# Rounding the first weight blocks by integer steps on three engines, with two split copies and a split sketch product, in a polysketch-attention and ELU kernel

## The chip, the cores and the metric

The kernel runs on one core of one Trainium2 chip. The metric is device time in microseconds, the median of several runs. The engines go by the names of the profile: PE (TensorE, with PEld for its weight loads), DVE (VectorE), ACT (ScalarE), POOL (GpSimd) and SP (SyncE, which issues most DMAs). Each takes its instructions in the order in which the program gives them.

## What is computed

```python
def phi(x):                                  # for q and k
    a = np.einsum('rd,bhsd->bhsr', S1, x)    # r = 8 sketch rows
    b = np.einsum('rd,bhsd->bhsr', S2, x)
    return outer(a, b)                       # 64 features per token
kv, z = phi(k)^T v, sum over s of phi(k)
attn = (phi(q) kv) / (phi(q) z + 1e-6)       # B = 4, H = 4, S = 1088, D = 32
x = attn as (4352, 128)                      # tokens x (heads * D)
h = x @ w_in                                 # 128 -> 2048
out = where(h > 0, h, exp(min(h, 0)) - 1) @ w_out
```

S1, S2, w_in and w_out come to the chip as 64-bit floats, two 32-bit words per value. The kernel makes 32-bit floats of them on the chip: this is the rounding that the change is about.

## The kernel before

The tokens are worked in groups of 512 (`g`), and w_in and w_out in eight blocks of 256 features (`cp`). For each pair the step is: h = x by w_in (`mm1`, 16 instructions into two PSUM tiles), e = exp on ACT (`elu_a`), gg = the ELU on DVE (`elu_d`), then gg by w_out (`mm2` and other forms of it for later groups). Groups 0 and 1 run interleaved while later inputs are still on their way; in `steps` the order is (0,0), (0,1), (1,0), (1,1), and so on. The schedule is manual: the program's order of calls is each engine's order of instructions, and the stretch that matters here, up to the first steps, is written out call by call at the end of the function.

The queries take this way to x, for groups 0 and 1:

- Sketch product: the transposed queries `qT` (a DVE transpose, L280) by the sketch matrix. Group 0 has `q1_first` (tile abqp, L505) and `q1z_first` (zqp, L517, the part for the denominators). Group 1 has `q1_second` (abwp, L526): eight products of 96 columns, on PE as sixteen instructions, and one ACT copy to the tile abw (L530). Both group-1 halves need the second DVE transpose of qT (128x576).
- `q2` = `q2_den` (pw, the sum and reciprocal den, an; L586 to L596) and `q2_out` (qp, in two halves, L609), all on DVE. `q2_den` takes a function `between` that is called after pw, and `q2_out` one between its halves; these slots hold the first step of a rounding (`RA`).
- `q4_early`: eight PE transposes of qp into two PSUM tiles qtp (L621), each copied by ACT to qpT (L622, 512 columns).
- `q5_early`: qpT by kvS, sixteen PE instructions into two PSUM tiles xps (L628), each copied by ACT to its half of the columns of xg (L634, 256 columns).

kvS, the attention state of batch 0, comes from `KA(0)` (kv, L435) and `KS_first` (an ACT copy kd, L481, a PE transpose, L482, an ACT copy kvS, L483). `keep_warm` issues PE products of constants into a tile that nobody reads.

Rounding of a block, in order: `RA` (DVE, L102: sign and mantissa masked away from the upper word, into W), `RB` (ACT, L107: the exponent rebased), `RS`, `RM`, `RD`, `RE` (all DVE, L117, L121, L129, L137: sign put in, mantissa of the upper word as a number, the lower word added to it, and the product of mantissa and exponent). `order` numbers the blocks: block 0 is w_in of cp 0, block 1 w_in of cp 1, block 2 w_out of cp 0. For blocks 0 and 1 the middle steps run once over both (`RC_2`). h of (0, 0) needs block 0, h of (0, 1) block 1, and the first product into the output tile o (`mm2(0, 0)`, L256) block 2, whose rounding `RA(2)`, `RB(2)`, `RC(2)` is written among the first steps.

The order around the change, after it `mm1_first` (h of group 0, block 0, in two halves of the columns w, as the halves of xg arrive):

```python
q2(1, 2, lambda: RA(2))
RB(2)
elu_a(0, 0, 0)
elu_a(0, 0, 1, (0,))
mm1(0, 1, (0,))
q4_early(1)
elu_d(0, 0, 0)
mm1(0, 1, (1,))
elu_a(0, 0, 1, (1,))
RC(2)
...
q5_early(1)
elu_d(0, 0, 1)
mm2(0, 0, True, False)
```

SP issues the loads in the order S1, k, q, v, w_in block 0, the rest of q, block 1, the two first w_out blocks, and the others. The functions that the diff touches, with the line numbers of the profile:

Of the kernel before, what the change touches and what calls it, by code (L numbers as in the profile page):

```python
# [12 lines left out]
F32 = mybir.dt.float32  # L13
ALU = mybir.AluOpType
U32 = mybir.dt.uint32
MUL, ADD, SUB, MAX = ALU.mult, ALU.add, ALU.subtract, ALU.max
AND, OR, SHL = ALU.bitwise_and, ALU.bitwise_or, ALU.logical_shift_left
EXP = mybir.ActivationFunctionType.Exp
RELU = mybir.ActivationFunctionType.Relu
AX = mybir.AxisListType.X  # L20


def _ap(ap: bass.AP, free):
    return dataclasses.replace(ap, ap=[list(ap.ap[0])] + [list(x) for x in free])
# [3 lines left out]
def kernel(  # L28
# [21 lines left out]
    nc = tc.nc  # L50
    B, H, S, D = q.shape
    R = S1.shape[0]
    P = 128
# [10 lines left out]
    const = ctx.enter_context(tc.tile_pool(name="const", bufs=1))  # L64
    work = ctx.enter_context(tc.tile_pool(name="wk", bufs=2))
    psum = ctx.enter_context(tc.tile_pool(name="psum", bufs=2, space=bass.MemoryType.PSUM))
# [27 lines left out]
    nc.vector.memset(ebias[:], -float(896 << 23))  # L94
    tiny = const.tile([P, 1], F32, name="tiny")
    nc.gpsimd.memset(tiny[:], 2.0 ** -20)

# [4 lines left out]
    def round_b(raw, dst, eng=nc.scalar):  # L104
        d = dst.bitcast(U32)
        if eng is nc.scalar:
            nc.scalar.activation(d, d, RELU, scale=8.0, bias=ebias[:dst.shape[0]])  # L107
        else:
# [3 lines left out]
    def words(raw):  # L112
        return (raw[:, :, 0], raw[:, :, 1]) if len(raw.shape) == 3 else (raw[:, :, :, 0], raw[:, :, :, 1])
# [5 lines left out]
    def round_m(raw, dst):  # L119
        hi = words(raw)[1]  # L120
        nc.vector.tensor_scalar(hi, hi, 0x000FFFFF, 0x00100000, op0=AND, op1=OR)  # L121

    def round_c(raw, dst):
        round_s(raw, dst)
        round_m(raw, dst)
# [15 lines left out]
    wide = S1.dtype != F32  # L141
# [12 lines left out]
    nc.vector.memset(warm[:], 0.0)  # L154
    nc.scalar.activation(warm[:], warm[:], EXP)

    W = const.tile([P, NP, 4 * P], F32, name="W")
    raw_w = {}
    if wide:
        raw_2 = const.tile([P, 2, 4 * P, 2], U32, name="raw")  # L160
# [18 lines left out]
    def round_w(f, i, *a):  # L179
        if wide:  # L180
            cp, w_in, w_out = order[i]
            c = slice(0 if w_in else 2 * P, 4 * P if w_out else 2 * P)
            f(raw_w[cp][:, c], W[:, cp, c], *a)

    def RA(i):
        round_w(round_a, i)

    def RB(i):
        round_w(round_b, i)


    def RC_2():
        if wide:
            for f in (round_s, round_m, round_d):
                f(raw_2[:, :, :2 * P], W[:, :2, :2 * P])

    def RS(i):
        round_w(round_s, i)
# [7 lines left out]
    def RE(i):  # L206
        round_w(round_e, i)
# [43 lines left out]
    width = [32]  # L251
# [8 lines left out]
    def keep_warm(n, cols=256, tile=P):  # L260
        ones = nc.const_aps.tensor(1.0, [P, 256], F32)
        for i in range(n):
            for c in range(0, P, tile):
                nc.tensor.matmul(idle[c:c + tile, :cols], ones[:, :tile], ones[:, :cols], skip_group_check=True,  # L264
                                 tile_position=(0, c))
# [222 lines left out]
    abw, ans, qp, qpT, xg, xps = {}, {}, {}, {}, {}, {}  # L488
# [7 lines left out]
    def half_tile(g, k):  # L496
        return (g // 2, 8 * (g % 2) + k) if g < NQ - 1 else (k, NT - 1)
# [20 lines left out]
                                 qT[b][:, t, :], SW[:, :, 2, :], skip_group_check=True, tile_position=(0, 64 * u))  # L518
        return p[:, :128].rearrange("p (t h r) -> p h t r", t=4, h=H)

    def q1_second():
        p = psum.tile([P, 512], F32, name="abwp", tag="h", bufs=4)
        for i in range(4):
            for u in range(2):
                b, t = half_tile(1, 2 * i + u)
                nc.tensor.matmul(p[64 * u:64 * u + 64, i * 96:i * 96 + 96], qT[b][:, t, :],  # L526
                                 SW[:].rearrange("p h x r -> p (h x r)"), skip_group_check=True,
                                 tile_position=(0, 64 * u))
        abw[1] = work.tile([P, H * 4, 3 * R], F32, name="abw1", tag="abq1", bufs=1)
        nc.scalar.copy(abw[1][:].rearrange("p (h t) y -> p h t y", h=H),  # L530
                       p[:, :384].rearrange("p (t h y) -> p h t y", t=4, h=H))


    units = {g: ([g, g + 1] if 4 <= g < NQ - 1 else [g]) for g in [2, 3] + list(range(4, NQ, 2))}
    un = {g: sum(qn[x] for x in gr) for g, gr in units.items()}
# [41 lines left out]
    def q2(g, parts=1, between=None):  # L577
        q2_den(g, None, between)
        q2_out(g, parts)

    def q2_den(g, zq=None, between=None):
        m = H * (un[g] if g > 1 else qn[g])
        x = abw[g][:, :m, :]
        pw = pws[g % 2]
        if zq is None:
            nc.vector.tensor_mul(pw[:, :m, :R], x[:, :, R:2 * R], x[:, :, 2 * R:3 * R])  # L586
        else:
            nc.vector.tensor_mul(pw[:, :m, :R].rearrange("p (h t) r -> p h t r", h=H),
                                 x[:, :, R:2 * R].rearrange("p (h t) r -> p h t r", h=H), zq)
        if between:  # L590
            between()
        den = work.tile([P, 8 * H], F32, name="den", tag="den")
        nc.vector.tensor_reduce(den[:, :m], pw[:, :m], axis=AX, op=ADD)
        nc.vector.reciprocal(den[:, :m], den[:, :m])
        an = work.tile([P, 8 * H, R], F32, name="an", tag="an")
        nc.vector.tensor_mul(an[:, :m], x[:, :, R:2 * R], _ap(den[:, :m], [[1, m], [0, R]]))  # L596
        ans[g] = an

    def q2_out(g, parts=1, between=None):
        m = H * qn[g]  # L600
        x, an = abw.pop(g), ans.pop(g)
        qp[g] = work.tile([P, 4 * H, R, R], F32, name="qp", tag="qp", bufs=2)
        for i in range(parts):
            if i and between:
                between()
            h = slice(i * m // parts, (i + 1) * m // parts)
            a_ = an[:, h]
            b_ = x[:, h, :R]
            nc.vector.tensor_mul(qp[g][:, h], _ap(a_, list(a_.ap[1:]) + [[0, R]]),  # L609
                                 _ap(b_, [b_.ap[1], [0, R], b_.ap[2]]))  # L610

    def q4_early(g):

        qpT[g] = work.tile([P, H, 2, P], F32, name="qpT", tag="qpT", bufs=2)
        for hh in range(2):
            p = psum.tile([P, 512], F32, name="qtp", tag="aux")
            for h2 in range(2):
                for m in range(2):
                    o = (h2 * 2 + m) * P
                    r = (2 * hh + h2) * 4 + 2 * m  # L620
                    nc.tensor.transpose(p[:, o:o + P], qp[g][:, r:r + 2].rearrange("p t i j -> p (t i j)"), ident[:])  # L621
            nc.scalar.copy(qpT[g][:, 2 * hh:2 * hh + 2], p[:].rearrange("p (h m s) -> p h m s", h=2, m=2))  # L622

    def q5_early(g):
        xp = [psum.tile([P, 512], F32, name="xps", tag="aux") for _ in range(2)]
        for h in range(H):
            for w in range(2):
                nc.tensor.matmul(xp[w][D * h:D * h + D, :256], kvS[64 * w:64 * w + 64, h, :],  # L628
                                 qpT[g][64 * w:64 * w + 64, h].rearrange("p m s -> p (m s)"),
                                 skip_group_check=True, tile_position=(64 * w, D * h))  # L630
        xg[g] = work.tile([P, 512], F32, name="xg", tag="xg", bufs=3)
        to = xg[g][:].rearrange("p (m w s) -> p w m s", w=2, s=P)
        for w in range(2):
            nc.scalar.copy(to[:, w], xp[w][:, :256].rearrange("p (m s) -> p m s", s=P))  # L634


    exch = [raw_2[:, c].bitcast(F32).rearrange("p (e m a) w -> p e m (a w)", e=2, a=16) if wide else
# [206 lines left out]
        for c in cs:  # L844
            quarters(hs[g, cp][c][:, :n], W[:, cp, c * P:c * P + P], xg[g][:, :n])

    def mm1_first():
        hs[0, 0] = [psum.tile([P, 512], F32, name="h", tag="h", bufs=4) for c in range(2)]
        for w in range(2):
            for c in range(2):  # L850
                cols = [x[:].rearrange("p (m w s) -> p w m s", w=2, s=P)[:, w] for x in (hs[0, 0][c], xg[0])]
                quarters(cols[0], W[:, 0, c * P:c * P + P], cols[1])

    def elu_a(g, cp, c, parts=(0, 1)):
# [5 lines left out]
        if 0 in parts:  # L860
            nc.scalar.activation(e, hs[g, cp][c][:, :n], RELU, scale=-1.0)  # L861
        if 1 in parts:
            nc.scalar.activation(e, e, EXP, scale=-1.0)  # L863

# [44 lines left out]
    def elu_last_a(k, parts=(0, 1)):  # L909
# [3 lines left out]
        if 0 in parts:  # L913
            nc.scalar.activation(e, hs["last", k][:, :2 * P], RELU, scale=-1.0)
        if 1 in parts:
            nc.scalar.activation(e, e, EXP, scale=-1.0)

# [39 lines left out]
    KO_first(7, KT)  # L957
    keep_warm(1, 96, 64)
    zq = q1z_first()
    q2_den(0, zq, lambda: RA(0))  # L960
    q2_out(0, 2, lambda: RA(1))
    KA(0)
    KS_first()
    keep_warm(1)
    RB(0)
    RB(1)
    q4_early(0)
    transp(qT, "q", 0, 8, NT)
    RC_2()
    RE(0)  # L970
    RE(1)
    q1_second()
    q5_early(0)
    keep_warm(1, 192, width[0])
    mm1_first()
    q2(1, 2, lambda: RA(2))
    RB(2)
    elu_a(0, 0, 0)
# [129 lines left out]
    for n in range(2, N):  # L1108
        g, cp = steps[n]
# [29 lines left out]
        g, cp = before  # L1139
# [10 lines left out]
    g = NQ - 2  # L1150
# [53 lines left out]
```

## Time and profile before

| what | us |
|---|---|
| median of 3 runs (lowest to highest) | 262.14 (261.85 to 262.18) |
| span of the profiled execution, first to last instruction | 260.57 |
| median less that span: what lies around it | 1.57 |
| PE, DVE, ACT, POOL busy in the span | 254.8, 186.9, 183.4, 159.0 |
| first h (`mm1_first`) on PE | 16.25 |
| group 1's pw on DVE | 16.35 |
| first product into o on PE | 21.58 |

The profile shows one execution. A timeline row gives the start, the time that the row takes, the engine, the line, the operation, the tiles written and read, the shape, and how many instructions are merged in it; in brackets stands the idle time of the engine ahead of the row and what ended it. [...]

### The profile page before, as it was taken

The page shows a single profiled execution, that of the slowest core. Times are in us where ns is not written, and L with a number is a line of the kernel's source. Part 1 is how long each engine was busy: PE and PEld are TensorE (multiplying, and loading weights), DVE is VectorE, ACT ScalarE, POOL GpSimd, SP SyncE. Part 2 cuts the span into 40 slices and gives each one's busy share as a digit, 9 for nine tenths or more (in the row PEclk, how much of TensorE's full clock was granted, in tenths as well). Part 3 has the DMA queues.
Part 4 walks back from the last instruction along what each step waited for, and adds up shares of the span by engine and source line. Part 5 has one row for each costly group of instructions (what it writes and reads, how often), then busy time and mean ns, then how long its engine had stood idle before and what let it go on. Part 6 is the DMA issues. An engine that isn't in the chain of part 4 may idle for free.

```text
span 260.6 us, 9756 instructions
## 1 busy us (share of the span) xinstructions
PE 254.8 (98%) x4123; PEld 158.4 (61%) x4123; DVE 186.9 (72%) x352; ACT 183.4 (70%) x358; POOL 159.0 (61%) x202
## 2 busy tenths in 40 slices
PE   8899999999999999999999999999999999999994
PEld 6753333453346667666666666665666666668993
DVE  6799999999988967997477675744466746544651
ACT  2379968766667577776687777775877777777792
POOL 3520007002179996788678798888688888887310
PEclk9999999999999999999999999999999999999999
DMA  5998079012112210002100204220001110110021
GB/s 173 330 358 222 3 223 268 24 21 85 28 18 28 31 34 18 3 15 34 20 0 4 33 10 104 60 30 13 3 3 27 34 26 3 25 19 3 3 30 33
DMA packets 30379, 15.61 MB, mean 60 GB/s; under 512 B 22496, under 2 KB 28000, under 8 KB 30336
## 3 DMA queue, kind: packets, MB, share of 16 engines
q1 hardware_dynamic: 29904, 14.63, 23.0%
q8 instruction: 32, 0.52, 0.9%
q10 hardware_dynamic: 368, 0.30, 0.3%
q0 software_dynamic: 64, 0.07, 0.1%
q14 instruction: 11, 0.09, 0.1%
HBM read 11.31 MB, written 2.36 MB: 52 GB/s over the span
## 4 chain that ended last, share of the span: by engine, by line
PE 97%; DVE 1%; ACT 0%; issue 0%; DVEq 0%
PE h L256 45%; PE pb L790 17%; PE pa L790 13%; PE o L256 5%; PE pb L766 4%; PE ol L256 3%; PE idle L264 1%; PE kv L435 1%; PE abp L343 1%; PE h L681 1%; PE h L551 1%; PE qtp L621 1%; DVE qp L609 1%; PE h L693 1%; PE xps L628 0%; PE kfps L365 0%
## 5 line engine op out<-in xcount | busy, mean ns | idle before, releaser
L256 PE MATMUL h<-xg,W 128*32 128x512 f32 (+3 forms) x904 | 130.8, 539 | 0.4 <-ACT xg L634 0.4
L869 DVE SCALAR_TENSOR_TENSOR gg<-e,h 128x512 f32<-128x512 f32 x128 | 85.9, 681 | 52.6 <-ACT e L863 47.8
L861 ACT ACTIVATE e<-h 128x512 f32<-128x512 f32 x128 | 75.5, 590 | 46.2 <-PE h L256 46.0
L863 ACT ACTIVATE e<-e 128x512 f32<-128x512 f32 x128 | 80.9, 632 | 3.8
L751 POOL TENSOR_TENSOR tt<-gg 128x512 f32<-128x512 f32 x50 | 64.3, 1286 | 28.9 <-DVE gg L869 25.2
L256 PEld LDWEIGHTS h<-xg,W 128*32 128x32 f32 (+1 forms) x904 | 43.0, 122 | 43.0 <-issue 34.4
L754 POOL TENSOR_TENSOR tt<-gg,tt 128x256 f32<-128x256 f32 x50 | 36.9, 739 | 3.9
L753 POOL TENSOR_TENSOR tt<-tt,gg 128x256 f32<-128x256 f32 x50 | 36.7, 734 | 3.9
L790 PEld LDWEIGHTS pa<-gg,W 128*64 128x64 f32 (+1 forms) x496 | 23.7, 126 | 22.4 <-issue 22.2
L790 PE MATMUL pa<-gg,W 128*64 128x128 f32 (+1 forms) x496 | 30.6, 274 | 0.0
L790 PE MATMUL pb<-tt,SS 128*64 128x128 f32 (+1 forms) x480 | 29.6, 273 | 0.0
L790 PEld LDWEIGHTS pb<-tt,SS 128*64 128x64 f32 (+1 forms) x480 | 22.8, 126 | 0.0
L790 PE MATMUL pa<-tt,SS 128*32 128x128 f32 (+1 forms) x288 | 21.2, 273 | 0.0
L790 PE MATMUL pb<-gg,SS 128*64 128x128 f32 (+1 forms) x256 | 19.9, 273 | 0.0
L790 PE MATMUL pb<-tt,W 128*64 128x128 f32 (+1 forms) x256 | 19.9, 273 | 0.0
L134 POOL TENSOR_TENSOR raw<-raw,tiny 128x512 f32<-128x512 f32 x1 | 1.0, 1041 | 24.7 <-DVE raw L129 24.7
L256 PE MATMUL o<-gg,W 128*32 128x512 f32 x128 | 15.3, 595 | 0.0
L790 PEld LDWEIGHTS pa<-tt,SS 128*32 128x32 f32 (+1 forms) x288 | 13.7, 124 | 0.0
L790 PEld LDWEIGHTS pb<-gg,SS 128*64 128x64 f32 (+1 forms) x256 | 12.8, 125 | 0.0
L790 PEld LDWEIGHTS pb<-tt,W 128*64 128x64 f32 (+1 forms) x256 | 12.8, 125 | 0.0
L766 PE MATMUL pb<-gg,W 128*32 128x256 f32 x192 | 11.5, 380 | 0.0
L921 DVE SCALAR_TENSOR_TENSOR gg<-e,h 128x256 f32<-128x256 f32 x16 | 6.6, 418 | 6.4 <-PE h L256 3.2
(163 smaller groups left out, 269.3 us busy)
## 6 DMA issues: line engine op xcount, KB each, us to landing
raw<-in_moe_w_in_dram SPq DMA_DIRECT2D x8, 256.0 KB, 6.3
raw<-in_moe_w_out_dram SPq DMA_DIRECT2D x8, 256.0 KB, 6.5
out_dram<-ob SPq DMA_DIRECT2D x112, 16.0 KB, 1.5
hd_k<-in_k_dram SPq DMA_DIRECT2D x3, 544.0 KB, 7.5
hd_q<-in_q_dram SPq DMA_DIRECT2D x3, 544.0 KB, 8.5
v<-in_v_dram SPq DMA_DIRECT2D x4, 288.0 KB, 7.1
v<-in_v_dram SPq DMA_DIRECT2D x4, 256.0 KB, 8.4
raw<-qpF SPq DMA_DIRECT2D x16, 64.0 KB, 2.0
```

What stands on the lines that cost most here:

```text
L256: nc.tensor.matmul(dst[c:c + tile], lhs[:, c:c + tile], rhs, skip_group_check=True, tile_position=(0, c), **kw)
L264: nc.tensor.matmul(idle[c:c + tile, :cols], ones[:, :tile], ones[:, :cols], skip_group_check=True, tile_position=(0, c))
L343: nc.tensor.matmul(ps[i // 5][64 * u:64 * u + 64, 64 * (i % 5):64 * (i % 5) + 64], kT[b][:, u * KT + i, :], Sab[:].rearrange("p h y -> p ( ...
L751: nc.gpsimd.tensor_tensor(_ap(t[:, 0], [[4 * P, 2], [P, 2], [1, P]]), _ap(gs[g, cp][:, 0, P:], [[4 * P, 2]] + us), _ap(gs[g, cp][:, 0], [[ ...
L753: nc.gpsimd.tensor_tensor(t[:, 1], t[:, 2], b11, op=ADD)
L754: nc.gpsimd.tensor_tensor(t[:, 3], b21, t[:, 1], op=SUB)
L766: nc.tensor.matmul(acc[1][0][r:r + width[0], 256 * hi:256 * hi + 256], lhs[:, w:w + width[0]], gg[:, c, 256 * u:256 * u + 256], start=(cp ...
L790: nc.tensor.matmul(bank[r:r + width[0], P * col:P * col + P], lhs[:, w:w + width[0]], rhs[:, u], start=(first and i in ((0,) if g == 1 els ...
L861: nc.scalar.activation(e, hs[g, cp][c][:, :n], RELU, scale=-1.0)
L863: nc.scalar.activation(e, e, EXP, scale=-1.0)
L869: nc.vector.scalar_tensor_tensor(gs[g, cp][:, c, :n], es[g, cp][:, c, :n], -1.0, hs[g, cp][c][:, :n], op0=ADD, op1=MAX)
L921: nc.vector.scalar_tensor_tensor(gs["last", k // 2][:, k % 2, :2 * P], es["last", k // 2][:, k % 2, :2 * P], -1.0, hs["last", k][:, :2 * P ...
```

## The change

For blocks 0 and 1 the rounding is replaced. With hi and lo the two words of a value, it is now: `strip`, hi without its sign into W (DVE for block 0, ACT's Abs for block 1); `floor`, the maximum of that and a small constant (POOL); `shift`, three bits to the left (DVE); `low`, lo scaled by 2^-51 plus 2.0, whose bits are the exponent's offset and the rounded low mantissa bits (ACT); `whole`, the integer sum of the two (POOL); and `round_s`, the sign (DVE, as before). `RA`, `RB`, `RC_2` and `RE` of these two blocks go.

The second copy of `q4_early(0)` is made by ACT and DVE, 256 columns each, and the second of the two copies of `q5_early(0)` by DVE. `q1_second` is cut in two: its first half stands after `q5_early(0)`, its second half and the one copy to abw stand inside `mm1_first`, between its two halves. The last `keep_warm` ahead of `mm1_first` has 64 columns instead of 192.

```diff
+    two = const.tile([P, 1], F32, name="two")
+    nc.gpsimd.memset(two[:], 2.0)
...
+    def strip(raw, dst, eng=nc.vector):
+        if eng is nc.vector:
+            nc.vector.tensor_scalar(dst.bitcast(U32), words(raw)[1], 0x7FFFFFFF, None, op0=AND)
+        else:
+            nc.scalar.activation(dst, words(raw)[1].bitcast(F32), ABS)
+
+    def floor(raw, dst):
+        nc.gpsimd.tensor_scalar_max(dst, dst, 2.0 ** -15)
+
+    def shift(raw, dst):
+        nc.vector.tensor_scalar(dst.bitcast(U32), dst.bitcast(U32), 3, None, op0=SHL)
+
+    def low(raw, dst):
+        lo = words(raw)[0]
+        nc.scalar.activation(lo.bitcast(F32), lo, IDENTITY, scale=2.0 ** -51, bias=two[:dst.shape[0]])
+
+    def whole(raw, dst):
+        nc.gpsimd.tensor_tensor(dst.bitcast(U32), dst.bitcast(U32), words(raw)[0], op=ADD)
...
-    def RC_2():
-        if wide:
-            for f in (round_s, round_m, round_d):
-                f(raw_2[:, :, :2 * P], W[:, :2, :2 * P])
+    R1 = round_w
...
-    def q1_second():
-        p = psum.tile([P, 512], F32, name="abwp", tag="h", bufs=4)
-        for i in range(4):
+    def q1_second(tiles):
+        if 1 not in abw:
+            abw[1, 0] = psum.tile([P, 512], F32, name="abwp", tag="h", bufs=4)
+            abw[1] = work.tile([P, H * 4, 3 * R], F32, name="abw1", tag="abq1", bufs=1)
+        p = abw[1, 0]
+        for i in tiles:
...
+        if 3 in tiles:
+            nc.scalar.copy(abw[1][:].rearrange("p (h t) y -> p h t y", h=H),
+                           p[:, :384].rearrange("p (t h y) -> p h t y", t=4, h=H))
...
-    def q4_early(g):
+    def q4_early(g, split=False):
...
+            if split and hh:
+                nc.scalar.copy(qpT[g][:, 2], p[:, :2 * P].rearrange("p (m s) -> p m s", m=2))
+                nc.vector.tensor_copy(qpT[g][:, 3], p[:, 2 * P:].rearrange("p (m s) -> p m s", m=2))
...
-            nc.scalar.copy(to[:, w], xp[w][:, :256].rearrange("p (m s) -> p m s", s=P))
+            (nc.vector.tensor_copy if split and w else nc.scalar.copy)(
+                to[:, w], xp[w][:, :256].rearrange("p (m s) -> p m s", s=P))
...
-    def mm1_first():
+    def mm1_first(between):
         hs[0, 0] = [psum.tile([P, 512], F32, name="h", tag="h", bufs=4) for c in range(2)]
         for w in range(2):
+            if w:
+                between()
...
     zq = q1z_first()
-    q2_den(0, zq, lambda: RA(0))
-    q2_out(0, 2, lambda: RA(1))
+    R1(strip, 0)
+    R1(floor, 0)
+    R1(low, 0)
+    q2_den(0, zq)
+    R1(strip, 1, nc.scalar)
+    R1(floor, 1)
+    R1(low, 1)
+    q2_out(0, 2)
+    for i in range(2):
+        R1(shift, i)
+        R1(whole, i)
     KA(0)
     KS_first()
     keep_warm(1)
-    RB(0)
-    RB(1)
-    q4_early(0)
+    q4_early(0, True)
     transp(qT, "q", 0, 8, NT)
-    RC_2()
-    RE(0)
-    RE(1)
-    q1_second()
-    q5_early(0)
-    keep_warm(1, 192, width[0])
-    mm1_first()
+    R1(round_s, 0)
+    q5_early(0, True)
+    R1(round_s, 1)
+    q1_second((0, 1))
+    keep_warm(1, 64, width[0])
+    mm1_first(lambda: q1_second((2, 3)))
     q2(1, 2, lambda: RA(2))
```

More of the change, by code (lines that the diff above doesn't have):

```diff
@@ L18 @@
 EXP = mybir.ActivationFunctionType.Exp
+IDENTITY = mybir.ActivationFunctionType.Identity
+ABS = mybir.ActivationFunctionType.Abs
 RELU = mybir.ActivationFunctionType.Relu
@@ L528, in q1_second @@
                                  tile_position=(0, 64 * u))
-        abw[1] = work.tile([P, H * 4, 3 * R], F32, name="abw1", tag="abq1", bufs=1)
-        nc.scalar.copy(abw[1][:].rearrange("p (h t) y -> p h t y", h=H),
-                       p[:, :384].rearrange("p (t h y) -> p h t y", t=4, h=H))
+        if 3 in tiles:
+            nc.scalar.copy(abw[1][:].rearrange("p (h t) y -> p h t y", h=H),
+                           p[:, :384].rearrange("p (t h y) -> p h t y", t=4, h=H))
     units = {g: ([g, g + 1] if 4 <= g < NQ - 1 else [g]) for g in [2, 3] + list(range(4, NQ, 2))}
@@ L621, in q4_early, with q5_early @@
                     nc.tensor.transpose(p[:, o:o + P], qp[g][:, r:r + 2].rearrange("p t i j -> p (t i j)"), ident[:])
-            nc.scalar.copy(qpT[g][:, 2 * hh:2 * hh + 2], p[:].rearrange("p (h m s) -> p h m s", h=2, m=2))
-    def q5_early(g):
+            if split and hh:
+                nc.scalar.copy(qpT[g][:, 2], p[:, :2 * P].rearrange("p (m s) -> p m s", m=2))
+                nc.vector.tensor_copy(qpT[g][:, 3], p[:, 2 * P:].rearrange("p (m s) -> p m s", m=2))
+            else:
+                nc.scalar.copy(qpT[g][:, 2 * hh:2 * hh + 2], p[:].rearrange("p (h m s) -> p h m s", h=2, m=2))
+    def q5_early(g, split=False):
         xp = [psum.tile([P, 512], F32, name="xps", tag="aux") for _ in range(2)]
```

## The prediction

> **What bounds the kernel now.** I read the page's parts 1 and 2 first. TensorE (PE) is busy for 98% of the span, and the granted clock has full height in every slice.
>
> ```profile
> span 260.6 us, 9756 instructions
> ...
> PE 254.8 (98%) x4123; PEld 158.4 (61%) x4123; DVE 186.9 (72%) x352; ACT 183.4 (70%) x358; POOL 159.0 (61%) x202
> ```
>
> So a change helps only if it takes idle time or work away from PE, and it hurts wherever it makes PE wait. The change lies between 9 and 18 us, so next I read the PE timeline there, then that of VectorE (DVE), in which the small share 72% hides a stretch that is full.
>
> ```profile
> 13.34 0.63 PE L621 MATMUL qtp<-ident,qp 128*128 128x128 f32 x4 [0.24 <-DVE qp L609]
> 13.93 0.88 PE L526 MATMUL abwp<-SW,qT 128*64 128x96 f32 x16
> 14.74 0.66 PE L628 MATMUL xps<-qpT,kvS 64*32 64x256 f32 x16
> 15.34 0.53 PE L264 MATMUL idle<-const-float32-1.0 128*32 128x192 f32 x8
> 16.25 2.79 PE L256 MATMUL h<-xg,W 128*32 128x256 f32 x40 [0.38 <-ACT xg L634]
> 18.97 1.09 PE L621 MATMUL qtp<-ident,qp 128*128 128x128 f32 x8
> 19.99 1.06 PE L256 MATMUL h<-xg,W 128*32 128x512 f32 x8
> 20.99 0.66 PE L628 MATMUL xps<-qpT,kvS 64*32 64x256 f32 x16
> 21.58 1.92 PE L256 MATMUL o<-gg,W 128*32 128x512 f32 x16
> ```
>
> Up to 16.25 PE follows a chain (qp, transposes, x, h). From 16.25 on no row has idle time before it: PE is the bound to the end.
>
> ```profile
> 12.50 0.69 DVE L609 TENSOR_TENSOR qp<-an,abq 128x512 f32<-128x512 f32 x1
> ...
> 15.68 0.76 DVE L137 SCALAR_TENSOR_TENSOR W<-raw,W 128x256 f32<-128x256 f32 x2
> 16.35 0.29 DVE L586 TENSOR_TENSOR pw<-abw 128x128 f32<-128x128 f32 x1
> ...
> 17.70 1.29 DVE L609 TENSOR_TENSOR qp<-an,abw 128x512 f32<-128x512 f32 x2
> ...
> 20.97 0.43 DVE L137 SCALAR_TENSOR_TENSOR W<-raw,W 128x256 f32<-128x256 f32 x1
> ```
>
> DVE is as full as PE: it is busy without a gap from 10.34 to 28.9. Its pw of group 1 (L586) starts when the rounding ends (16.44, less the usual overlap of 0.09), not when its input comes, which was there at 15.34 (ACT's copy L530, 14.86 + 0.48). The last view is the list of waits between 8 and 24 us, and its decisive line is a small one:
>
> ```profile
> PEld o L256 <- DVE W L137: 0.4, 1, 0.4
> ```
>
> The first product into o (21.58) needs the w_out block whose rounding ends on DVE at 20.97 + 0.43 = 21.40. Its weight load waited for that, while PE was still in xps. **PE and DVE meet here without slack**: what makes DVE late between 16.35 and 21.40 arrives on PE nearly undiminished.
>
> **The change, part by part.** Times are of the profiled execution: span 260.57, where the runs have 262.14 in the median. The 1.57 between lies around the span, and I carry it along.
>
> *qp of group 0.* RA(0) and RA(1) leave DVE. The reduction L593 began at 10.75 and could begin at 10.63 + 0.03: −0.09. The second L609 began at 12.50 instead of 12.30: −0.20. strip(0) (0.29, the row of L102 with the same form; block 0 has landed by 9.43) lies in the 0.23 in which L588 waited for PE, plus one overlap: 0. So qp ends at 12.90 instead of 13.19.
>
> *ACT's new work.* low(0), strip(1), low(1) stand ahead of the copy kd (L481), which ran at 11.43 after 1.90 us idle. Block 1 lands at 10.94 by my count: the queue reuses eight landing marks in turn, and its issue at 10.96 is the eighth after block 1's (5.23). Abs isn't in the trace; it lies between a 256-column copy (L634: two in 0.65, so 0.28 from start to start) and L107 (two in 0.91, so 0.40). I take the copy, since neither has a bias tile. low has L107's form: 0.51. strip(1) runs from 10.97, low(1) 11.25 to 11.76, kd from 11.70: +0.27 (with the other end +0.39, with a later landing more). The idle time doesn't cover this, because it was idle time before a landing. kd leads to PE's transpose, kvS and then, in PE's order, the qtp transposes: the first four move from 12.44 to 12.71, the second four, one every 0.109, follow at 13.20 and end at 13.80, instead of 13.96. Of the 0.29 won on DVE 0.16 is left.
>
> *The split copies.* The second qpT copy took ACT 0.59; two halves take 0.37 there and 0.28 to 0.42 on DVE (L938, 128 columns from PSUM; L921, 256 columns: I take 0.42, the same width). ACT ends the first copy at 14.0 and its half at 14.28, DVE its own at 14.25, instead of 14.59: −0.31. xps follows 0.16 behind: 14.44 to 15.11. The first xg half is copied from 15.20 to 15.57, and the second no longer stands between it and h: that and the above give h at 15.67 instead of 16.25, **−0.58**. DVE runs the q transpose to 15.0, round_s(0) to 15.3 and its xg half to 15.7, which h's second part needs at 16.9. The dropped keep-warm columns lie in PE's waiting time: 0.
>
> *Rounding.* RC_2 and two RE (0.65 + 0.43 + 0.69 + 0.76) leave DVE; two shifts (0.17 at L110's 16x32 to 0.29; I take 0.29) and two round_s (0.42, L117 at this width) come. On GpSimd (POOL) floor lies between 0.23 (L304, 64 columns) and 0.74 (L753, two inputs); from L304 to the 0.29 of 128 columns (masks) it grows by 0.06 per 64: I take 0.41. whole lies between 0.66 (half of L135, which also reads every other word) and 1.31; I take 0.74: whole(0) ends near 13.9, whole(1) near 14.7. W isn't late until whole(0) ends after 15.15, so both ends cost nothing. Sxp, SWs, qE and zh now stand behind these four on POOL and end near 17; the first to need any is kfps at 37.4. No DMA moves.
>
> *The sketch product of group 1 (q1_second).* Before, it ran at 13.93, under the wait for qpT. Now its first half follows the q transpose at 15.0, its second half stands behind h's first part (0.86), and the one copy to SBUF waits for both. So: h 15.67, + 0.86 = 16.53, + 0.55 for eight of the sixteen (0.30 of starts + 0.25) = 17.08, + 0.03 and the copy 0.48 = 17.59, + 0.03: pw at 17.62 instead of 16.35, **+1.27**. This is the wait that the change adds. Behind pw on DVE stand, in order, RA(2), den, an, both qp, elu_d and the whole rounding of block 2; RB(2) on ACT and all after it follow RA(2). DVE, eased by some 0.7 us, idles from about 16.1 to 17.6.
>
> *On PE.* h and the eight other products keep it busy to 18.6. The qtp of group 1 needs the first qp, 18.40 + 1.27 = 19.67, so PE idles 1.1 us. h resumes at 20.93 (+0.94). The product into o needs block 2, 21.40 + 1.27 = 22.67, 0.18 more as before: 22.85, **+1.27**. ACT, gapless from 18.4 to 32.3, has the same delay. Nothing later gives it back, as PE has no idle row there. With some hundredths absorbed I take +1.25: span 261.8, time 262.14 + 1.25 = **263.4**. The ends (kd 0.12 later or 0.1 earlier; pw reached 0.3 sooner or later) give 263.0 to 263.9 for this case.
>
> **A rule against the row.** L117 with 512 columns took 1.72 at 44.26, 0.67 elsewhere:
>
> ```profile
> 44.26 1.72 DVE L117 SCALAR_TENSOR_TENSOR W<-raw,W 128x512 uint32<-128x512 uint32 x1
> ```
>
> ```profile
> 42.81 2.62 POOL L322 TENSOR_TENSOR kp<-abk 128x1280 f32<-128x1280 f32 x1
> ```
>
> It ended 0.55 after POOL's long instruction (45.43), so it seems to have stood still until then. The Trainium skill, "SBUF — State Buffer", section "Who interferes with whom", says as much: a DVE instruction with two SBUF inputs and a GpSimd instruction that reads SBUF exclude each other, and the second waits for all of the first. That speaks against floor(1), as the next rival shows.
>
> **Rivals.** (1) *POOL gets in first.* floor(1) is ready at about 11.35 while an runs (11.29 to 11.58), and both qp have two SBUF inputs. If POOL starts between an and qp, qp waits up to 0.41: qp ends at 13.31, the second qtp start at 13.45 instead of 13.20: +0.25, time 263.65. For it: the row above. Against: DVE queues its next instruction 0.03 behind the last. (2) *The late product is hidden: faster.* Then only h's −0.58 is left: 261.6. This decides at one point: ACT's abw copy would have to end by 15.8, and it stands behind h's first part. For it: DVE has less to do. Against: the rows give 17.6. (3) *No change*: pw is reached some 0.9 sooner than I reckon, and what DVE loses is caught up: about 262.2. (4) *An operation is dear.* A POOL integer add above 1.9 us pushes h, 3 us each giving about +1.1 more: 264.5. Or Abs or Identity makes ACT reload its table: the trace has one load, 1.28 us at 2.06, and Copy, Relu and Exp need no second. Two loads (there and back), one ahead of low(0), mostly hidden by the wait for the landing, one ahead of the exponential, give about +1.3 more: 264.7. The Trainium skill, "ScalarE: Activation LUTs", section "Table sets", counts both functions among those that every set holds, which would leave no load.
>
> **How the numbers follow.** Forecast 0.60, (1) 0.19, (4) 0.06: all slower. (3) 0.08; (2) 0.07. 0.2% is 0.52 us, about what a measurement here tells from nothing. Faster 0.07, same 0.08, slower 0.85. The range goes from 262.5 to 264.2: it holds the forecast, (1) and the upper part of (3), and leaves out (2), (4) and the rest of (3), under 2 in 10.
>
> **What would show it.** The first h near 15.7 (range 15.4 to 16.0); before the pw of group 1 an idle DVE of about 1.5 us, ended by ACT's abw copy; a PE gap near 1.1 us before the second qtp, released by qp; the first product into o near 22.85, and the same PE rows behind it. kd near 11.7 shows the landing; an L609 longer than 0.7 shows rival (1). The prediction is wrong if pw starts before 17.0, or if o starts at 21.6 although pw is late.

## The result, and the profile after

| | before | after |
|---|---|---|
| median of 5 runs (lowest to highest), us | 261.85 (261.73 to 262.18) | 263.58 (263.49 to 264.27) |
| ratio, 95% interval | | 1.0067 (1.0055 to 1.0080) |
| span of the profiled execution | 260.57 | 261.85 |

The change makes the kernel slower by 0.7%, 1.73 us between the medians. The first view is the PE timeline of the changed kernel over the stretch that was shown of before (lines moved down by 20 to 26: L276 is h and o, L549 abwp, L643 qtp, L654 xps).

```profile
12.41 1.03 PE L643 MATMUL qtp<-ident,qp 128*128 128x128 f32 x8
13.68 1.40 PE L654 MATMUL xps<-qpT,kvS 64*32 64x256 f32 x16 [0.24 <-ACT qpT L648]
15.10 0.55 PE L549 MATMUL abwp<-SW,qT 128*64 128x96 f32 x8
15.58 0.32 PE L284 MATMUL idle<-const-float32-1.0 128*32 128x64 f32 x8
15.72 1.05 PE L276 MATMUL h<-xg,W 128*32 128x256 f32 x16
16.70 0.55 PE L549 MATMUL abwp<-SW,qT 128*64 128x96 f32 x8
17.18 1.93 PE L276 MATMUL h<-xg,W 128*32 128x256 f32 x24
20.00 1.23 PE L643 MATMUL qtp<-ident,qp 128*128 128x128 f32 x8 [0.89 <-DVE qp L631]
21.16 1.07 PE L276 MATMUL h<-xg,W 128*32 128x512 f32 x8
22.16 0.66 PE L654 MATMUL xps<-qpT,kvS 64*32 64x256 f32 x16
22.75 1.92 PE L276 MATMUL o<-gg,W 128*32 128x512 f32 x16
```

h starts 0.53 sooner than before (15.72 instead of 16.25), and yet o starts 1.17 later (22.75 instead of 21.58). The 0.53 is not the change's. This execution was ahead by 0.59 already at zqp, a product that the change doesn't touch (before, then after):

```profile
9.57 0.66 PE L517 MATMUL zqp<-SW,qT 128*64 128x32 f32 x16 [0.17 <-DVE SW L465]
8.98 0.66 PE L537 MATMUL zqp<-SW,qT 128*64 128x32 f32 x16 [0.17 <-DVE SW L485]
```

Counted from zqp, h takes 6.74 instead of 6.68, and o 13.77 instead of 12.01. That is 1.76 more, about the 1.73 between the medians. Between h and o stands what the kernel before did not have: PE idles 0.89 ahead of the second qtp, until DVE has qp of group 1. The DVE timeline shows why qp is late:

```profile
13.94 0.42 DVE L646 COPY qpT<-qtp 128x256 f32<-128x256 f32 x1 [0.94 <-ACT qpT L645]
...
15.61 0.47 DVE L121 SCALAR_TENSOR_TENSOR W<-raw,W 128x256 uint32<-128x256 uint32 x1
17.81 0.29 DVE L608 TENSOR_TENSOR pw<-abw 128x128 f32<-128x128 f32 x1 [1.73 <-ACT abw L553]
...
22.26 0.42 DVE L160 SCALAR_TENSOR_TENSOR W<-raw,W 128x256 f32<-128x256 f32 x1
```

pw of group 1 waits 1.73 us for ACT's copy of the sketch product; before, it waited for nothing. It starts 1.46 later, qp of group 1 follows it, and the second qtp starts at 20.00 instead of 18.97. From there to o the PE timeline has no idle time: the h behind that qtp starts 1.17 later (21.16 instead of 19.99), and o has the same 1.17.

The rounding of block 2 (L160) ends at 22.68 instead of 21.40, 0.07 ahead of o (0.18 before). In the list of waits the weight load of o still has the row it had before:

```profile
PEld o L276 <- DVE W L160: 0.4, 1, 0.4
```

This row doesn't show that block 2 held o. It is the same 0.4 in e3 and e8 below, where pw came sooner than before, and in every kernel here o starts 0.59 to 0.60 behind the xps just ahead of it.

From the start of o to the end there are 239.11 us after and 238.99 before. All of the loss lies ahead of o, in the first 23 us.

### The profile page after: what moved, and what is told of

It reads as the page before. It is cut to its first block, busy times and chain, and to the rows that moved or that the text cites. A ratio compares the mean times of both kernels' runs of the same rounds, so it can differ in the third digit from the quotient of the medians.

```text
span 261.9 us, 9762 instructions
## 1 busy us (share of the span) xinstructions
PE 254.7 (97%) x4123; PEld 157.9 (60%) x4123; DVE 186.4 (71%) x352; ACT 183.4 (70%) x358; POOL 162.1 (62%) x207
## 4 chain that ended last, share of the span: by engine, by line
PE 92%; DMA 2%; SPq 2%; ACT 1%; DVE 1%; issue 0%
PE h L276 44%; PE pb L817 17%; PE pa L817 13%; PE o L276 5%; PE pb L793 4%; PE ol L276 3%; DMA raw<-in_moe_w_in_dram 2%; PE kv L455 1%; PE h L708 1%; SPq L81 1%; PE h L573 1%; PE qtp L643 1%; PE h L720 0%; PE kfps L385 0%; PE xps L654 0%; SPq L89 0%
## 5 line engine op out<-in xcount | busy, mean ns | idle before, releaser
L276 PE MATMUL h<-xg,W 128*32 128x512 f32 (+3 forms) x904 | 131.0, 539 | 0.0
L276 PEld LDWEIGHTS h<-xg,W 128*32 128x32 f32 (+1 forms) x904 | 42.8, 122 | 42.3 <-issue 34.6
L276 PE MATMUL o<-gg,W 128*32 128x512 f32 x128 | 15.4, 595 | 0.0
```

Of the source, the lines that this page charges most:

```text
L276: nc.tensor.matmul(dst[c:c + tile], lhs[:, c:c + tile], rhs, skip_group_check=True, tile_position=(0, c), **kw)
```

## The experiments

Theory: the late sketch product of group 1 makes the loss, through pw on DVE. Rivals: the new rounding makes it (A), or the split copies are what matters (B). Each kernel was timed beside the kernel before, whose median in these comparisons was 261.85 to 261.93. Executions don't all start alike (the last section), so times inside the profile are also read from zqp, a product ahead of all that the kernels differ in, and from kd, ACT's copy at the head of the chain to x. "o to end" is nearly the same in all of them. "zqp to o", less the 12.01 of before, gives what the medians give within 0.13, but for e7, whose profiled execution was the slowest of its five runs.

| kernel | zqp | kd | first h | pw | first o | zqp to o | o to end | median | ratio to before (95%) |
| --- | --- | --- | --- | --- | --- | --- | --- | --- | --- |
| before | 9.57 | 11.43 | 16.25 | 16.35 | 21.58 | 12.01 | 238.99 | 261.85 | |
| changed | 8.98 | 11.51 | 15.72 | 17.81 | 22.75 | 13.77 | 239.11 | 263.58 | 1.0067 (1.0055 to 1.0080) |
| e1 | 8.87 | 11.42 | 15.96 | 16.45 | 21.39 | 12.52 | 239.08 | 262.35 | 1.0025 (1.0011 to 1.0039) |
| e2 | 9.10 | 10.97 | 15.79 | 17.90 | 22.84 | 13.74 | 239.10 | 263.71 | 1.0066 (1.0054 to 1.0078) |
| e3 | 8.95 | 11.41 | 15.70 | 15.15 | 21.03 | 12.08 | 238.97 | 261.90 | 1.0004 (0.9993 to 1.0014) |
| e4 | 9.68 | 12.50 | 16.37 | 18.45 | 23.39 | 13.71 | 239.08 | 263.56 | 1.0059 (1.0046 to 1.0072) |
| e5 | 9.35 | 11.22 | 15.70 | 15.15 | 21.14 | 11.79 | 239.09 | 261.68 | 0.9992 (0.9983 to 1.0001) |
| e6 | 8.89 | 11.48 | 17.07 | 17.02 | 22.40 | 13.51 | 239.02 | 263.28 | 1.0056 (1.0044 to 1.0069) |
| e7 | 8.89 | 11.93 | 17.14 | 17.10 | 22.48 | 13.59 | 239.01 | 262.94 | 1.0039 (1.0026 to 1.0051) |
| e8 | 9.13 | 11.00 | 15.27 | 14.85 | 20.61 | 11.48 | 239.00 | 261.47 | 0.9981 (0.9966 to 0.9996) |
| e9 | 9.00 | 10.87 | 15.49 | 14.88 | 20.79 | 11.79 | 239.01 | 261.58 | 0.9991 (0.9979 to 1.0003) |

**e1, the sketch product whole again**

```diff
-    q1_second((0, 1))
+    q1_second((0, 1, 2, 3))
     keep_warm(1, 64, width[0])
-    mm1_first(lambda: q1_second((2, 3)))
+    mm1_first(lambda: None)
```

> The changed kernel with group 1's sketch product whole again, all of it behind x's products (xps) and ahead of the first h; rounding and split copies stay. Theory (the late sketch product makes the loss): the abw copy ends near 16.5 instead of 17.78, group 1's pw starts near 16.5 instead of 17.81, the first product into o near 21.6 instead of 22.75; time 262.4 (1.1 to 1.2 under the changed kernel's 263.58). Rival A (the new rounding makes the loss, by POOL's floor and by ACT standing behind the landing of block 1): pw may start sooner, but the time stays at 263.2 or more.

As the theory had it: 262.35, 1.23 less than the changed kernel, though still 0.25% above the kernel before. h comes later than there (15.96 instead of 15.72), and o still comes 1.36 sooner, because pw does. In its DVE and PE timelines the wait shrinks and the gap is gone:

```profile
16.45 0.29 DVE L608 TENSOR_TENSOR pw<-abw 128x128 f32<-128x128 f32 x1 [0.40 <-ACT abw L553]
```

```profile
18.65 1.22 PE L643 MATMUL qtp<-ident,qp 128*128 128x128 f32 x8
```

**e2, the split of the sketch product alone, in the kernel before**

```diff
-    q1_second()
     q5_early(0)
-    keep_warm(1, 192, width[0])
-    mm1_first()
+    q1_second((0, 1))
+    keep_warm(1, 64, width[0])
+    mm1_first(lambda: q1_second((2, 3)))
```

> The kernel before with only the sketch product of group 1 split around x (and 64 instead of 192 keep-warm columns); old rounding, old copies. Theory: pw starts near 18.2 instead of 16.35, and nothing hides it: time 261.85 + 1.7 = 263.5. Rival A: the sketch product isn't what costs: 261.6 to 262.2.

263.71: the whole loss (1.0066, where the changed kernel has 1.0067), without any of the new rounding or copies. pw waits 1.92 for the abw copy, and PE idles 0.89 ahead of qtp, as in the changed kernel:

```profile
17.90 0.29 DVE L588 TENSOR_TENSOR pw<-abw 128x128 f32<-128x128 f32 x1 [1.92 <-ACT abw L533]
```

```profile
20.09 1.23 PE L623 MATMUL qtp<-ident,qp 128*128 128x128 f32 x8 [0.89 <-DVE qp L611]
```

The shorter keep-warm has no part in it: PE idles 0.23 behind it, ahead of h. Rival A falls for the main part.

**e3, the new rounding alone**

```diff
-    q4_early(0, True)
+    q4_early(0)
...
     R1(round_s, 0)
-    q5_early(0, True)
     R1(round_s, 1)
-    q1_second((0, 1))
-    keep_warm(1, 64, width[0])
-    mm1_first(lambda: q1_second((2, 3)))
+    q1_second()
+    q5_early(0)
+    keep_warm(1, 192, width[0])
+    mm1_first()
```

> The kernel before with only the new rounding of blocks 0 and 1; the sketch product whole at its old place, ACT makes all copies. Theory: VectorE is idle ahead of pw, which starts near 15.5, h near 15.9 to 16.2: 261.4 to 262.0, no loss. Rival A: floor on POOL (0.86 and 1.22 in the changed kernel's trace) and the late kd copy delay x: 262.5 or more.

261.90, no difference to before. pw starts at 15.15, 1.2 sooner than before, but in the kernel before PE was not waiting for it: the first qp of group 1 ended at 18.40 there, and qtp began at 18.97. So only an earlier x would bring something, and kd is as late as in the changed kernel: 2.46 behind zqp (2.53 there, 1.86 before). What e3 and e1 differ in, the split copies with the sketch product behind x, costs 0.45.

**e4, ACT makes all copies, the sketch product stays split**

```diff
-    q4_early(0, True)
+    q4_early(0)
...
-    q5_early(0, True)
+    q5_early(0)
```

> The changed kernel with ACT making all of the qpT and xg copies of group 0, as before; rounding and split sketch product stay. In the changed kernel's trace VectorE's half copy of qpT began only when ACT's ended (13.94 behind 13.91), so the two halves took 0.83 where one copy took 0.59. Theory (the halves run one behind the other, and the split gains nothing): h starts within 0.15 of 15.72, time 263.4 to 263.7. Rival B (the split copies shorten the way to x by 0.5): h later by 0.3 to 0.5, time 263.9 to 264.1.

263.56, as the theory had it. The start of h missed its expectation (16.37), since the profiled execution was the slowest of this kernel (264.25) and block 1 landed 1.0 later in it (kd at 12.50). From kd, h takes 3.87, against 4.21 in the changed kernel: with the split copies h came 0.34 later, not sooner, and rival B falls. The 0.34 is there already at the start of the sketch product (15.10 there, 15.75 here), which in the changed kernel waits for the transpose that DVE makes behind its half copy. Why the median shows nothing of the 0.34 is not settled; the lowest run, 263.07, lies 0.42 below the changed kernel's lowest.

**e5, block 1 behind**

```diff
-    R1(strip, 1, nc.scalar)
-    R1(floor, 1)
-    R1(low, 1)
     q2_out(0, 2)
-    for i in range(2):
-        R1(shift, i)
-        R1(whole, i)
+    R1(shift, 0)
+    R1(whole, 0)
     KA(0)
     KS_first()
     keep_warm(1)
+    R1(strip, 1, nc.scalar)
+    R1(floor, 1)
+    R1(low, 1)
...
     R1(round_s, 0)
-    R1(round_s, 1)
+    R1(shift, 1)
+    R1(whole, 1)
...
-    q2(1, 2, lambda: RA(2))
+    q2(1, 2, lambda: (RA(2), R1(round_s, 1)))
```

(against e3)

> The kernel with the new rounding alone (ACT makes all copies, sketch product whole at its old place), and block 1's steps moved: strip and low of block 1 on ACT behind kd and kvS, its floor, shift and whole behind those of block 0, its sign step behind the first step of block 2. Reason: with the new rounding kd started only at 11.41, behind ACT's two steps of block 1, which had waited for its landing (10.65), while PE idled 0.96; and floor of block 1 on POOL ran 1.29 beside the two qp (1.49 for two instead of 1.29). Theory (those two hold x back, by 0.3 to 0.4 together): kd near 10.8, the two qp in 1.29, h 0.3 to 0.4 earlier than in the kernel with rounding alone; time 261.4 to 261.7, under the kernel before. Rival C (x is held by something else, or the start's scatter is larger): 261.8 to 262.1.

261.68 is as far as expected, but the interval reaches no change. The mechanism shows: kd now follows KA, 1.87 behind zqp instead of 2.46, h takes 6.35 from zqp instead of 6.75, and the two qp take 1.29 again. (The start of h itself, 15.70, is that of e3, because this execution began 0.40 later.) The new collision is seen in the timelines of DVE and POOL:

```profile
15.15 0.85 DVE L606 TENSOR_TENSOR pw<-abw 128x128 f32<-128x128 f32 x1 [0.16 <-ACT abw L550]
```

```profile
15.12 0.73 POOL L144 TENSOR_TENSOR W<-W,raw 128x256 uint32<-128x256 uint32 x1 [0.46 <-ACT abw L550]
```

pw takes 0.85, where it takes 0.29 elsewhere, and ends 0.15 behind POOL's sum.

**e6, the new rounding with the split copies, the sketch product ahead of xps**

```diff
-    q4_early(0)
+    q4_early(0, True)
...
-    q5_early(0)
+    q5_early(0, True)
```

(against e3)

> The new rounding with the split copies, the sketch product whole at its old place (ahead of xps). Theory (VectorE's half of qpT waits for ACT's half, and the transpose of the later queries, the sign steps and the sketch product stand behind it on VectorE and PE): x later by 0.5 to 0.9 than with rounding alone; time 262.4 to 262.9. Rival B (the split copies shorten the way to x): 261.3 to 261.7.

The direction held, the size did not: 263.28. From kd, h takes 5.59 against 4.29 in e3, 1.30 more. DVE's half of qpT starts at 13.91, the transpose of the later queries behind it at 14.25, and the sketch product, which needs these queries and stands ahead of xps, leaves PE idle for 1.66:

```profile
13.50 0.38 ACT L643 COPY qpT<-qtp 128x256 f32<-128x256 f32 x1
13.91 0.42 DVE L644 COPY qpT<-qtp 128x256 f32<-128x256 f32 x1 [1.01 <-ACT qpT L643]
```

```profile
15.08 0.88 PE L546 MATMUL abwp<-SW,qT 128*64 128x96 f32 x16 [1.66 <-DVE qT L300]
```

The changed kernel escapes this because its sketch product comes after xps.

**e7, a PSUM tile for each half**

```diff
+            ps = [p, psum.tile([P, 512], F32, name="qtp2", tag="h", bufs=4) if split and hh else p]
...
-                    nc.tensor.transpose(p[:, o:o + P], qp[g][:, r:r + 2].rearrange("p t i j -> p (t i j)"), ident[:])
+                    nc.tensor.transpose(ps[h2][:, o:o + P], qp[g][:, r:r + 2].rearrange("p t i j -> p (t i j)"), ident[:])
...
-                nc.vector.tensor_copy(qpT[g][:, 3], p[:, 2 * P:].rearrange("p (m s) -> p m s", m=2))
+                nc.vector.tensor_copy(qpT[g][:, 3], ps[1][:, 2 * P:].rearrange("p (m s) -> p m s", m=2))
```

(against e6)

> New rounding and split copies, sketch product whole ahead of xps, as in the kernel with rounding and copies (263.28), but the transposes that VectorE copies go into a PSUM tile of their own. In that kernel VectorE's copy began at 13.91, 0.03 behind the end of ACT's copy from the same tile (13.88). Theory (the two halves run one behind the other because they read one PSUM tile): VectorE's half starts within 0.1 of ACT's, h 0.3 to 0.45 earlier, time 262.8 to 263.0. Rival (the order comes from the tile that both write, or VectorE is late for another reason): 263.2 to 263.4.

262.94, 0.34 less than e6, and h at 5.21 from kd instead of 5.59. In its timeline, DVE and ACT run side by side, and DVE waits for PE:

```profile
13.90 0.42 DVE L645 COPY qpT<-qtp 128x256 f32<-128x256 f32 x1 [0.75 <-PE qtp L642]
13.95 0.38 ACT L644 COPY qpT<-qtp 128x256 f32<-128x256 f32 x1
```

So it was the shared PSUM tile that set the halves one behind the other; both still write one qpT tile.

**e8, block 1 last, and e9, the same with e7's split copies**

```diff
-    R1(shift, 0)
+    transp(qT, "q", 0, 8, NT)
+    R1(shift, 0)
...
-    transp(qT, "q", 0, 8, NT)
     R1(round_s, 0)
-    R1(shift, 1)
-    R1(whole, 1)
...
-    q2(1, 2, lambda: (RA(2), R1(round_s, 1)))
+    q2_den(1, None, lambda: (R1(shift, 1), RA(2), R1(whole, 1)))
+    R1(round_s, 1)
+    q2_out(1, 2)
```

(e8 against e5)

> The kernel with block 1's steps moved behind (261.68), with the transpose of the later queries ahead of block 0's shift, and block 1's shift and whole behind group 1's pw, its sign step ahead of qp. There POOL's whole of block 1 (15.12 to 15.85) stood beside pw, which took 0.85 instead of 0.29. Theory (PE is the bound and pw has slack; the sketch product ahead of xps starts 0.2 sooner): 261.5 to 261.7, pw back at 0.29. Rival (block 1's sign step is now too late for h of block 1, needed near 17.3): 261.9 or more.

> As the last, with the second qpT copy split between ACT and VectorE from two PSUM tiles. Theory (the halves now run side by side and end 0.2 sooner, and x follows): 261.3 to 261.6. Rival (the sketch product on PE ahead of xps sets x by then): no difference to the last, 0.1 at most.

e8 takes 261.47, with pw back at 0.28, and is the only kernel here whose interval (0.9966 to 0.9996) lies below the kernel before, if narrowly; the gain is 0.2%. e9, at 261.58, adds nothing: its sketch product ends on PE at 14.30 and xps starts at 14.23 behind it, so the earlier qpT has no use. Of the change, the rounding brings a little if it stands where nothing waits for it; the split sketch product costs, and the split copies brought nothing in any of these kernels.

## Why the prediction was right

*The late sketch product* was the cause, as forecast. Its four marks came near where the working put them: pw at 17.81 (17.62 said), a wait of 1.73 ahead of it (1.5), a PE gap of 0.89 (1.1) released by qp, o at 22.75 (22.85). e1 and e2 show it as cause and not only as company: making it whole again brings back 1.23 us, splitting it alone in the kernel before costs all of the loss.

*No slack between PE and DVE at o*: this step does not hold. The working let o wait for block 2 (22.67), while PE's own way to o, through qtp and h, was to be 0.94 late. In the changed kernel PE's own way is 1.17 late, and this is all of o's delay; block 2 was ready 0.07 to 0.18 ahead of o in every kernel. DVE and PE meet at qtp instead. Before, the first qp of group 1 ended 0.57 ahead of qtp (18.40, 18.97); in the changed kernel qtp follows it by 0.15 (19.85, 20.00). So there was slack: pw came 1.46 later and o 1.17. Whether block 2 would have held o had PE been sooner, no run shows.

*The sum*: between the two spans it is +1.28, where +1.25 was said. Between the medians it is +1.73. The profiled execution of before was a late one: its span is 260.57, while before's runs beside e1 to e4 have 260.1 in most cases, so 1.57 was too little for what lies around the span (1.73 to 1.83 in those runs). From zqp, where the late start drops out, the working has 13.28 to o, and the changed kernel took 13.77, 0.49 more:

| stretch | said | measured |
|---|---|---|
| zqp to kd | 2.13 | 2.53 |
| kd to h | 3.97 | 4.21 |
| h to pw | 1.95 | 2.09 |
| pw to o | 5.23 | 4.94 |

The time itself, 263.4 against 263.58, came nearer than the change did, and that part is luck: the median it started from was 0.29 too high (262.14, where five runs have 261.85), and the change 0.48 too small.

*kd behind the landing of block 1*: the mechanism is right, the size too small. kd came at 11.51 (11.70 said), behind ACT's steps of block 1, which the landing at 10.74 released. But from zqp it came 0.67 later than before (2.53 instead of 1.86), where the working has 0.27. The landing follows the loads and not PE: between the two executions zqp moved by 0.59 and the landing by 0.20 (10.94 to 10.74), so worked out from an execution whose PE began late, the wait looked short. In e5 and e8, whose ACT makes kd ahead of these steps, kd is again 1.87 behind zqp. The first row is of the changed kernel, the second of e5:

```profile
10.76 0.43 ACT L131 ACTIVATE W<-raw 128x256 f32<-128x256 f32 x1 [0.82 <-DMA raw<-in_moe_w_in_dram]
```

```profile
11.22 0.27 ACT L501 COPY kd<-kv 128x128 f32<-128x128 f32 x1 [0.77 <-PE kv L455]
```

The first four transposes, too, were read wrongly: before, they followed the first qp (12.38, start at 12.44) and not kd. From kd they start 1.01 behind there, and 0.90 in the changed kernel.

*The split copies*, −0.31: wrong. The two halves were put side by side, but DVE's began 0.03 behind the end of ACT's: 0.83 from the first start to the last end, where one copy took 0.59. e7 shows that the shared PSUM tile is the reason. I had not weighed what the Trainium skill, "PSUM — Partial Sum Buffer", section "PSUM bank collisions raise a hardware error", says: the compiler's scheduler adds an order between any two instructions on different engines that touch one bank in the same group of 32 partitions, reads included. e6 and e7 agree with it (13.91 behind 13.88 with one tile, 13.90 beside 13.95 with two); whether that scheduler made the order here, no run shows.

*h at 15.67* came out (15.72) by two errors that cancel, which is luck: kd came 0.19 sooner than said, in an execution that began sooner, and from kd to h it took 0.24 more, with the late copies. The gain of 0.58 on the kernel before is not there: counted from zqp, h comes 0.06 later.

I also took h of the kernel before to wait for the second xg copy. It waited for block 0. Before, and in e2 with the old rounding and ACT's copies, h starts 0.15 behind the end of block 0's rounding (16.10 and 16.25, 15.64 and 15.79), and in e2 PE's wait ahead of h is put down to the rounding (L137). So it takes the new rounding, and not the split copy of xg, to be rid of this wait: in e3, where ACT makes both copies, PE has no idle time ahead of h.

*POOL*, floor at 0.41: too small by half. floor(0) took 0.86 with no DVE instruction beside it that reads two SBUF tiles.

*Rival (1), POOL beside qp*: it was there, as an addition. The two qp took 1.49 instead of 1.29, and floor(1) 1.22 instead of 0.86. In e5 and e8, with floor elsewhere, the qp are back at 1.29. The second qp, begun at 11.71, did not stand still until floor(1) ended at 12.49, as it took only 0.88 in all. Beside POOL's sums DVE was held much longer: pw in e5 took 0.85 and ended 0.15 behind the sum, and block 0's sign step in e3 took 0.95 instead of 0.42 and ended 0.28 behind it. The rule of the Trainium skill, "SBUF — State Buffer", section "Who interferes with whom", by which one of the two waits for all of the other, thus fits the steps beside the sums, and not those beside the maximum.

*Rival (4)*: no operation was dear enough to matter. The sums took 0.74 or less each, Abs 0.43 and the step with Identity 0.55 and 0.51, and there is still one table load. That agrees with the Trainium skill, "ScalarE: Activation LUTs", section "Table sets".

## What to carry to other kernels

Before moving work off a busy engine, look for its next input: when VectorE was relieved, what mattered was when its next operand came, and the change had just moved that operand's producer behind another stage. A small product that feeds a long chain on another engine belongs ahead of the large product, even if PE then starts the large one a little later (e1: h 0.24 later, time 1.2 less). When work on a PSUM tile is split between two engines, look whether the halves really ran side by side: here they did only with a PSUM tile for each half (e7). And compare single executions from a point ahead of the change: from zqp to o they gave the loss of the medians (1.76, 1.73), where the two spans gave 1.28.

## What the runs showed of the hardware that was not expected

- The first record of full TensorE clock lies anywhere from 3.75 (e4) to 6.93 us (before) in these executions, though the first instructions are the same. In the kernel before, the products of abp start 0.11 apart until then and 0.06 apart behind it. ACT's step that waits for block 1's landing also moves, from 10.65 (e3) to 11.76 (e4). And zqp starts between 8.87 (e1) and 9.68 (e4), though the change and the experiments don't touch the way to it: before and e2, which are the same up to there, have 9.57 and 9.10.
- POOL is no cheaper with one input than with two: the maximum of 128x256 with a constant took 0.86 with nothing in its way (block 0 in e3 and e5), the integer sum of two such tiles, one read at every other word, 0.73 to 0.74 (e5).
- What POOL does to a DVE instruction with two SBUF inputs depended on POOL's instruction. Beside the integer sum (two inputs) DVE stood nearly still, as told above. Beside the maximum (one input), of which POOL still had 0.78 to do, block 0's sign step in e5 took 0.61 instead of 0.42 and ended first; in e8 pw took its usual 0.28 (14.85 to 15.13) although the maximum ran until 15.10. Which property of the two POOL instructions decides, no run shows. The rows are of e5:

```profile
13.88 0.61 DVE L121 SCALAR_TENSOR_TENSOR W<-raw,W 128x256 uint32<-128x256 uint32 x1 [0.23 <-POOL W L144]
```

```profile
13.81 0.85 POOL L134 TENSOR_SCALAR W<-W 128x256 f32<-128x256 f32 x1
```
